# Normalising on Pool by add and multiply, modulation weights queued behind two token tiles, and a new order

**Chip, cores, metric.** One core of one Trainium2 chip. The metric is the device time of one execution in microseconds (us). Executions of one kernel scatter by about 1%, so medians are quoted, and kernels are compared by a ratio: the mean time of one kernel's fast runs over that of the other's fast runs of the same rounds, so not quite the ratio of the quoted medians. One experiment round shares one chip; the kernel before was run again in each.

## The reference

A transformer block with adaptive layer norm, sliding-window attention and an MLP over the token axis; S = 2048 tokens, D = 512, 32 heads of 16, window 256, F = 1792, all bf16.

```python
sa, ca, ga, sb, cb, gb = split(silu(c) @ w_mod)          # six vectors of 512
h = layernorm(x) * (1 + ca) + sa                         # norm l1
x = x + ga * (attention(h @ wqkv) @ wo)                  # causal, last 256 keys
h = layernorm(x) * (1 + cb) + sb                         # norm l2
x = x + gb * transpose(gelu(layernorm(h)^T @ w1 + b1) @ w2 + b2)   # norm l3
```

## The kernel before

The engines are called as in the profile: PE is TensorE (matmuls; PEld its weight loads), DVE VectorE, ACT ScalarE, Pool GpSimd, and SP (SyncE) issues most of the transfers (DMA). The kernel records some 1350 small operations and emits them in a fixed order, a list of numbers with the engine as a letter (A, D, P for ACT, DVE, Pool). Every engine then works through its own queue in that order: in the trace of the change the input of PE's transposition of the silu is ready at 5.85 us, and it starts at 7.31, behind the 14 products listed ahead of it. Tokens come in 16 tiles of 128, four tiles to a group G. Scores are exponentiated on ACT in 75 pieces (`et`), attention products go to `pxy`, projections to `pq` (queries, keys) and `pv` (values, copied into the cleared tiles `VT`), the first MLP product to `pu`. Each tile is normalised three times: `xn` before the projections, `n2` (also called xn) before the second modulation, `hb` before the MLP.

```python
    for v in (0, 1):       # modulation weights of the first norm, 512 KB each
        o_wm[v] = load(f"wm{v}", wmod[:, :, v*D:(v+1)*D], wm_v[:, :, v*D:(v+1)*D], 512 * KBT, -29.0 + 0.1 * v, eng="ACT")
    for t in range(2):     # two token tiles, 128 KB each, on SP's queue
        o_x[t] = load(f"x{t}", xres[t][:], x_dram[t*P:(t+1)*P, :], 128 * KBT, -30.0 + 0.01 * t)
    ...
        def e_rs(e, a, b):                   # 1/std on ACT
            mv, rs = box[box_key]
            ac.activation(out=rs[:, a:b], in_=mv[:, a:b, 1], func=ACT.Ln, bias=eps_t[:], scale=1.0)
            ac.activation(out=rs[:, a:b], in_=rs[:, a:b], func=ACT.Exp, scale=-0.5)
    ...
    def normalize(e, dst, src, key, i):      # on DVE or Pool, as the order says
        mv, rs = box[key]
        (ve if e == "DVE" else po).tensor_scalar(
            out=dst, in0=src, scalar1=mv[:, i, 0:1], scalar2=rs[:, i : i + 1],
            op0=ALU.subtract, op1=ALU.mult,
        )
    # VT[r] cleared by DVE or Pool:
    vt_zero = [op("vz", {"DVE": 1.7, "POOL": 4.3}, lambda e, r=r: (ve if e == "DVE" else po).memset(VT[r][:], 0.0), pos=-20.0 + 5 * r) for r in range(3)]
    ...  # keys split by parity, on Pool: multiply and add
    (ve if e == "DVE" else po).tensor_scalar(out=dst, in0=view, scalar1=mask_par[:, par : par + 1], scalar2=0.0, op0=ALU.mult, op1=ALU.add)
```

The softmax here doesn't subtract the row's maximum and nothing guards it: scores larger than these inputs give would overflow.

Of the kernel before, what the change touches and what calls it, by code (L numbers as in the profile page):

```python
# [45 lines left out]
48 3 0 4 45 2 55 78D 7 1 35 8 39 5 47 6 31 9 82 56 41 81 10 37 11 57 32 12 58 43 13 36 14 83 50 15 34 16 59 84 54 17  # L46
60 18 46 61 42 88D 19 63 89D 20 62 21 92 22 64 33 23 95 93D 53 94D 24 97A 40 96D 38 25 104 85 105 26 107 106A 108 27
52 109A 110D 28 111 86 29 112 30 183 113A 114D 119 87 120 122 184 121D 123 49 124D 130 131 310 125 115 126 132A 116
185 90P 187 118D 117A 134 135 136 188 91P 127 137D 128 44 129D 138 133 139 98 140D 189 195 99D 141 101 100D 196 51
142 103D 186 102D 190 311 143 144 191 203 197 145D 161 312 192 162 204 65 163D 193 146 165 66 147 164 211 205 80P  # L50
148D 194 212 149D 198 313 174 177 175 178 199 176D 218 179D 200 154 213 201 155 219 202 157D 150 151 156D 206 180
314 152D 181 158 220 159 153D 222 207 208 160D 169 223 209 170 166 74 167 171D 210 182 214 315D 224 226 316D 168D
215 317P 67 227 79P 318D 323 68 324 216 234 228 217 319 326D 235 320 221 325D 225 322D 229 522 236 238 230 69 321D
239 172 71 173 70 240 245 72 231 339 75 246 340 232 362 342D 363 341A 523 249 247 330 364D 250 331 327 332D 328 524
334 251 253 354 329D 254 355 525 335 233 356D 526 261 255 336 357 262 343 338D 358 344 337D 237 333 241 263 345D 265
242 346D 351 243 754 266 370 371 244 352 372D 376 267 353D 373 248 377 252 366 256 347 365 257 380 378 374 348 381
359 360 258 384 382 259 76 385 260 350D 264 268 349D 269 392 77 386 361D 367 393 368 73 992 272 369D 375 993 273 994
270 527D 396 996 394 271 528P 997 274 397 379 995 383 529P 755 998 387 530D 388 403 398 284 275 404 276 531 277 532
389 407 405 390 535 534D 408 536 391 533D 395 537D 399 285 409 411 400 538D 281 412 282 278 283 279 401 413 419 280
539 420 402 540 286 566 756 423 421 567 424 287 406 541D 410 414 288 757 430 425 289P 542 568D 431 543 563 544D 564  # L60
415 290D 432 434 291P 416 555 435 556 417 565D 418 422 292D 758 558D 438 293P 436 557D 551 439 552 546 426 553D 294P
427 554D 446 440 579 295P 301 447 559 296P 580 428 450 581D 448 560 297D 451 571 429 298D 572 302 457 452 573D 433
458 562D 437 441 299D 561D 442 300P 461 459 303 574 462 569 575 547 443 465 463 444 304 466 445 449 453 576D 548 454
577 467 473 550D 455 545 487 474 488 456 578 549D 460 464 305 468 475 477 308D 306D 469 484 478 489 309P 485 307P
582 486 583 470 570 479 588 587 471 759D 589 472 476 760D 496 480 761P 493 481 584D 590 762P 593 482 490 591 594 483
497 491 492 598 595 494 599 495 498 607 600 592 608 499 767 763 768 601 764 500 612 596 609 613 501D 597 502D 602
770D 503P 765D 603 620 614 769D 504P 621 766D 513 783 586 787 615 604 625 505D 622 784 610 626 788 785D 585 605 786D
630 627 606 506D 631 611 789D 507P 616 790D 617 639 628 632 795 508D 640 774 633 775 796 623 618 509D 644 641 619
510P 797D 645 624 629 514 511P 634 776D 635 652 646 512P 771 515 653 772 777 773D 642 636 657 654 637 779 516 658
638 780 647 1000 782D 517 662 659 643 518D 520D 663 648 521D 1001 519D 781D 649 671 664 1005 672 1002 1003 1006  # L70
1004D 650 676 673 665 1007 677 798 660 1008 799 651 655 684 678 1009D 656 685 661 674 666 679 716 800D 667 689 668
801 1011 686 669 717 690 778 670 718 675 802 680 694 691 1016 695 692 1012 687 1017 681 703 696 1013 704 1014 697
1018 1019 1015D 682 708 705 683 791 1020D 709 792 688 794D 693 706 698 710 820 793D 699 719 821 720 811 721 812 700
825 822 813D 806 826 701 807 711 702 808D 707 823 827 830 728 712 831 814 828 815 803 713 816D 714 839 832 804 818
715 725 840 805D 819 809 726 824 833 844 841 829 727 817 845 834 729 810 722 723 835 1022 724 836 852 846 1023 730
853 1024 1027 731 1025 854 857 847 1028 1026D 858 1029 855 1033 837 1030 842 732 862 1032 859 733D 838 1021 863 843
734D 1010 1031D 848 1034 735D 849 736D 871 864 1038 737D 872 865 1035 1039 1040 738D 850 739D 876 873 860 1036 877
1041 851 740P 1037D 856 861 745 741P 878 866 884 1042D 867 1044 885 746 1045 1049 742D 1050 868 747 886 889 1051 869
890 1046 874 1052 743D 1047 744D 891 879 894 1048D 870 895 875 748 880 1055 1053D 881 903 749 892 1056 882 750D 1060
896 752D 1061 904 751D 1057 883 1058 887 1062 1059D 905 1063 753D 908 1064A 1065 897 1077 1054 909 948 1043 949 999  # L80
1078 950 910 916 1079 888 917 893 960 898 951 906 899 952 918 911 921 961 953 1080 922 968P 1081 1083 1082 969P 1084
900 962 926 923 1086 970P 927 901 1087 1085 902 907 919 963 980 912 935 913 1088 1066 928 1067 936 929 1068 1069
971D 1089 924 914 1090 1070A 915 972P 940 937 1091 920 941 938 925 930 973D 1092 982 931 1095 932 1093 942 933 1096
981 943 934 939 1094 944 988D 1097 1098 945 1119 1122 983 1099 1128 946 1101 1127 989P 1100 1102 947 954 1103 955
1150 956 957 958 964 1071 1072 959 965 1073 966 974P 1074 1104 1076 975D 1105 967 1123 976D 1142 1075A 1120 977D
1134 1126 1106 978P 1138 1121 1107 984 1124 1108 1129 1110 979D 1130 985 1109 1125 1111 990P 1133 1162 986 1131 1113
1132 1114 1112 987 1146 991D 1116 1115 1135 1147 1136 1143 1139 1137 1117 1140 1163 1151 1141 1144 1166 1148 1167
1154 1118 1149 1170 1152 1158 1159 1153 1174 1145 1155 1178 1156 1182 1179 1160 1186 1161 1164 1175 1171 1157 1190
1165 1200 1168 1201 1169 1172 1210 1211 1173 1176 1212 1187 1180 1183 1181 1213 1184 1202 1177 1230 1240 1188 1220
1189 1203 1250 1185 1231 1221 1222 1214 1204 1191 1205 1223 1192 1251 1224 1193 1270 1194 1252 1195 1206 1241 1196  # L90
1242 1197 1215 1232 1198 1253 1207 1260 1254 1208 1271 1233 1209 1261 1199 1234 1280 1272 1273 1225 1216 1274 1217
1226 1281 1227 1262 1235 1218 1282 1219 1290 1236 1300 1237 1275 1276 1243 1283 1244 1245 1263 1264 1265 1284 1285
1301 1246 1291 1247 1255 1310 1238 1320 1248 1239 1302 1256 1228 1249 1303 1257 1229 1266 1304 1267 1321 1330 1277
1292 1311 1268 1305 1278 1286 1293 1258 1322 1312 1287 1259 1331 1279 1294 1269 1295 1313 1332 1296 1306 1297 1314
1333 1307 1315 1298 1323 1316 1288 1299 1324 1334 1317 1289 1340 1308 1325 1326 1309 1335 1327 1341 1336 1318 1342
1337 1343 1319 1344 1328 1345 1338 1346 1347 1339 1329 1348 1349
# [55 lines left out]
def kernel(  # L152
# [173 lines left out]
    for v in (0, 1):  # L326
        o_wm[v] = load(f"wm{v}", wmod[:, :, v * D : (v + 1) * D], wm_v[:, :, v * D : (v + 1) * D], 512 * KBT, -29.0 + 0.1 * v, eng="ACT")
# [134 lines left out]
    def norm_ops(tag, tiles, deps, poss, box_key, parts):  # L462
        st_ops, rs_of = [], {}

        def e_stat(e, i):
            if i == 0:
                box[box_key] = (
                    small.tile([P, 4, nc.vector.BN_AGGR_DIM], F32, name="mv", tag=tag + "mv"),
                    small.tile([P, 4], F32, name="rs", tag=tag + "rs"),
                )  # L470
            st = small.tile([P, nc.vector.BN_STATS_DIM], F32, name="st", tag=tag + "st")
            ve.bn_stats(out=st[:], in_=tiles(i)[:])
            ve.bn_aggr(out=box[box_key][0][:, i, :], in_=st[:])

        def e_rs(e, a, b):
            mv, rs = box[box_key]
            ac.activation(out=rs[:, a:b], in_=mv[:, a:b, 1], func=ACT.Ln, bias=eps_t[:], scale=1.0)
            ac.activation(out=rs[:, a:b], in_=rs[:, a:b], func=ACT.Exp, scale=-0.5)

        for i in range(4):  # L480
            prev = [st_ops[-1]] if st_ops else []
            st_ops.append(op(f"{tag}st", {"DVE": 0.82}, lambda e, i=i: e_stat(e, i), deps=deps[i] + prev, pos=poss[i]))
            for a, b in parts:
                if b == i + 1:
                    o = op(f"{tag}rs", {"ACT": 0.46}, lambda e, a=a, b=b: e_rs(e, a, b), deps=st_ops[:], pos=poss[i])
                    for k in range(a, b):
                        rs_of[k] = o
# [641 lines left out]
```

## Time and profile before

| | before |
|---|---|
| median of its runs | 285.25 us (three runs, 283.94 to 286.07; 284.8 with a fourth) |
| span of the profiled run | 282.6 us |
| PE, DVE, ACT, Pool busy | 88%, 74%, 66%, 34% |
| normalisations on Pool, each | 2090 ns (14), 2147 ns (4) |
| modulation product starts | 9.73 us |

In the profile a row has engine, operation, output and inputs, and how often it occurs (x14). "Idle before" is the engine's wait ahead of these instructions, and the arrow names what ended it. An engine that is 34% busy can still set the time: what counts is who waits for it. Six of Pool's normalisations, 12.4 us, stand in the chain that ended last. The lines themselves are shown in the prediction.

### The profile page before, as it was taken

The numbers are of one execution on the slowest core, as the hardware profiler recorded it, in microseconds if no ns is written. First come the engines' busy times: TensorE is split into PE (matmuls) and PEld (weight loads), VectorE is DVE, ScalarE is ACT, GpSimd is POOL, SyncE is SP. The second block draws the span as 40 slices with busy tenths as digits, with TensorE's granted clock in tenths as the row PEclk, the third lists the DMA queues.
The fourth block names the chain that finished last, engine by engine and source line by source line (L and its number), as shares of the span: only waits on it lengthen the run. The fifth ranks groups of instructions, "written<-read, shape, count | busy, mean of one in ns | idle before, by whom it ended". The sixth has DMA issues, their size and how long they took to land.

```text
span 282.6 us, 10503 instructions
## 1 busy us (share of the span) xinstructions
PE 249.7 (88%) x4693; PEld 140.1 (50%) x4737; DVE 209.7 (74%) x428; ACT 186.5 (66%) x279; POOL 96.1 (34%) x132
## 2 busy tenths in 40 slices
PE   8787969999699998665799999999799999999993
PEld 2464746656557664442455444545444444444441
DVE  7464998858677779999786889988988770332765
ACT  2074988999679999995999999899832661000000
POOL 8745790344007559695020041105226000000000
PEclk9797999999979999999999999999999999999999
DMA  7997000002930000000000006219057960010222
GB/s 197 345 348 155 6 2 3 2 5 68 295 91 5 5 5 3 2 2 2 2 3 2 5 2 177 52 35 266 3 173 280 410 252 2 0 56 0 98 73 74
DMA packets 31445, 24.80 MB, mean 88 GB/s; under 512 B 6056, under 2 KB 29608, under 8 KB 31400
## 3 DMA queue, kind: packets, MB, share of 16 engines
q1 hardware_dynamic: 30336, 23.08, 27.1%
q10 hardware_dynamic: 1064, 1.05, 1.2%
q8 instruction: 37, 0.61, 0.9%
q14 instruction: 8, 0.07, 0.1%
HBM read 22.03 MB, written 2.10 MB: 85 GB/s over the span
## 4 chain that ended last, share of the span: by engine, by line
PE 54%; DVE 18%; ACT 12%; POOL 8%; issue 4%; DMA 3%; POOLq 0%; DVEq 0%
PE pu L192 27%; ACT et L192 9%; PE pxy L192 8%; PE pq L192 6%; PE psa L192 6%; POOL xn L192 4%; DVE VT L192 4%; DVE et L192 3%; PE pa L192 3%; POOL h L192 2%; DMA wmod<-in_w_mod_dram 2%; DVE xn L192 2%; DVE h L192 2%; PE pv L192 2%; ACT lz L192 2%
## 5 line engine op out<-in xcount | busy, mean ns | idle before, releaser
L192 ACT ACTIVATE et<-psa 128x1536 bf16<-128x1536 f32 x75 | 109.0, 1453 | 11.5 <-PE psb L192 6.4
L192 PE MATMUL pu<-hb,w1p 128*128 128x512 bf16 x213 | 52.2, 380 | 2.0 <-DMA w1p<-in_B_w_dram 0.7
L192 PE MATMUL pu<-guT,w 128*128 128x512 bf16 x219 | 48.4, 379 | 0.3
L192 ACT ACTIVATE et<-psb 128x512 bf16<-128x512 f32 x75 | 44.8, 598 | 0.0
L192 PE MATMUL pxy<-et,VT 128*32 128x192 bf16 (+3 forms) x960 | 37.7, 235 | 6.4 <-DVE OT L192 5.5
L192 POOL TENSOR_SCALAR KT<-kb,mask_par 128x512 bf16<-128x512 bf16 (+1 forms) x36 | 23.1, 655 | 56.4 <-DVE kb L192 52.8
L192 POOL TENSOR_SCALAR xn<-x,mv,rs 128x512 bf16<-128x512 bf16 x14 | 29.2, 2090 | 36.4 <-ACT rs L192 34.3
L192 PE MATMUL pxy<-et,ones_bd 128*32 128x192 bf16 (+3 forms) x960 | 37.8, 234 | 0.0
L192 PE MATMUL pq<-h1T,wqkv 128*128 128x512 bf16 (+1 forms) x147 | 33.7, 343 | 2.9 <-DVE VT L192 1.6
L192 PE MATMUL psa<-QT,KT 32*128 32x192 bf16 (+3 forms) x720 | 30.3, 233 | 5.8 <-ACT et L192 4.9
L192 PEld LDWEIGHTS <-w 128*128 128x128 bf16 x224 | 21.9, 98 | 26.4
L192 PEld LDWEIGHTS <-w1p 128*128 128x128 bf16 x224 | 20.1, 98 | 26.3 <-issue 3.0
L192 PEld LDWEIGHTS <-VT 128*32 128x32 bf16 x960 | 24.7, 97 | 13.0 <-issue 11.6
L192 DVE SCALAR_TENSOR_TENSOR o<-pu,b2FM,bc_gb 128x512 f32<-128x512 f32 x16 | 11.8, 749 | 24.3 <-PE pu L192 24.1
L192 PE MATMUL psb<-QT,KT 32*128 32x192 bf16 (+3 forms) x240 | 29.7, 234 | 0.0
L192 DVE TENSOR_TENSOR et<-et,maskt 128x512 bf16<-128x512 bf16 (+2 forms) x56 | 28.0, 532 | 2.2 <-ACT et L192 2.2
L192 PEld LDWEIGHTS <-KT 32*128 32x128 bf16 x960 | 15.4, 93 | 28.0 <-issue 25.6
L192 PEld LDWEIGHTS <-ones_bd 128*32 128x32 bf16 x960 | 23.6, 98 | 0.1
L192 DVE CAST VT<-pv 64x512 bf16<-64x512 f32 x29 | 19.8, 688 | 3.2 <-PE pv L192 2.7
L192 DVE BATCH_NORM_STATS2 st<-x 128x6 f32<-128x512 bf16 x32 | 21.7, 679 | 0.2
L192 PEld LDWEIGHTS <-wqkv 128*128 128x128 bf16 x160 | 14.0, 100 | 15.2 <-issue 5.3
L192 PE MATMUL pv<-wqkv,h1T 128*32 128x256 bf16 x512 | 17.8, 274 | 1.2 <-DVE VT L192 0.6
(90 smaller groups left out, 353.2 us busy)
## 6 DMA issues: line engine op xcount, KB each, us to landing
w1p<-in_B_w_dram SPq DMA_DIRECT2D x14, 512.0 KB, 6.4
w<-in_B_w_dram SPq DMA_DIRECT2D x14, 512.0 KB, 8.8
x<-in_A_x_dram SPq DMA_DIRECT2D x16, 128.0 KB, 6.4
wmod<-in_w_mod_dram SPq DMA_DIRECT2D x4, 512.0 KB, 6.9
out_dram<-otile SPq DMA_DIRECT2D x16, 128.0 KB, 1.7
wmod<-in_w_mod_dram ACTq DMA_DIRECT2D x2, 512.0 KB, 5.7
wqkv<-in_A_wqkv_dram SPq DMA_DIRECT2D x2, 384.0 KB, 6.1
wqkv<-in_A_wqkv_dram SPq DMA_DIRECT2D x1, 512.0 KB, 7.1
```

The source lines that it names most:

```text
L192: ins = call(*args, **kwargs)
```

## The change

Its intent: Pool had been given normalisations in the belief that they cost 0.7 us there. The change gives Pool a form that does cost about that (add the negated mean, multiply by 1/std), computes the negated means `nm`, corrects the costs, derives a new order of all operations from them, and moves the two weight loads to the queue of the token tiles.

```diff
-        o_wm[v] = load(..., 512 * KBT, -29.0 + 0.1 * v, eng="ACT")
+        o_wm[v] = load(..., 512 * KBT, -29.0 + 0.1 * v)
...
+        def e_nm(e, a, b):
+            mv, _, nm = box[box_key]
+            (ve if e == "DVE" else po).tensor_scalar(
+                out=nm[:, a:b], in0=mv[:, a:b, 0], scalar1=-1.0, scalar2=0.0, op0=ALU.mult, op1=ALU.add)
...
     def normalize(e, dst, src, key, i):
+        mv, rs, nm = box[key]
+        if e == "DVE":
+            ve.tensor_scalar(out=dst, in0=src, scalar1=mv[:, i, 0:1], scalar2=rs[:, i : i + 1], op0=ALU.subtract, op1=ALU.mult)
+        else:
+            po.tensor_scalar(out=dst, in0=src, scalar1=nm[:, i : i + 1], scalar2=rs[:, i : i + 1], op0=ALU.add, op1=ALU.mult)
...
-op("xn", {"DVE": 0.325, "POOL": 0.7}, ...)
+op("xn", {"DVE": 0.325, "POOL": 0.77}, ...)
...   # likewise n2, hb; two-input c2, s2: POOL 1.0 -> 1.17; the last group's l2, l3 kept off Pool, but hb allowed there
...   # ORDER: a new list throughout; VT's first clearing 78D -> 78P
```

## The prediction

> **What bounds the kernel now.** I read the busy times first, then the same by stretch, then the costliest forms on Pool, then the chain that ended last, and last the queues around its longest pieces.
>
> ```profile
> PE 249.7 (88%) x4693; PEld 140.1 (50%) x4737; DVE 209.7 (74%) x428; ACT 186.5 (66%) x279; POOL 96.1 (34%) x132
> ```
>
> PE is busy for 249.7 of 282.6 us. No matmul is added or removed, so the time is about PE's work plus PE's idle time, 32.9 us. The stretches show where that lies (columns: stretch and length, PE, PEld, DVE, ACT, POOL busy, granted clock, DMA share, GB/s):
>
> ```profile
> 0.00:9.70 9.70, 6.63 (x17) 2.15 (x17) 6.35 (x16) 2.09 (x4) 8.67 (x49) 1.00 0.84 240
> 14.00:40.00 26.00, 22.74 (x545) 15.88 (x546) 19.11 (x40) 19.86 (x31) 16.81 (x15) 0.93 0.53 141
> 112.00:131.00 19.00, 11.45 (x326) 7.58 (x327) 17.81 (x35) 17.25 (x23) 15.63 (x10) 1.00 0.01 2
> 131.00:165.00 34.00, 31.06 (x765) 17.57 (x771) 27.98 (x61) 31.37 (x44) 5.56 (x8) 1.00 0.01 3
> 205.00:219.30 14.30, 13.73 (x119) 6.27 (x119) 11.91 (x27) 4.35 (x16) 6.98 (x4) 1.00 0.66 231
> 219.30:278.20 58.90, 58.62 (x267) 26.50 (x271) 30.67 (x47) 10.52 (x15) 0.40 (x1) 1.00 0.28 108
> ```
>
> After 205 us PE is full (72.4 of 73.2 us): nothing another engine does there matters. Before 9.7 us PE runs only warm-up products. The loss in between is largest at 112 to 131 us: 7.55 us idle, while DVE, ACT and Pool are nearly full. Elsewhere ACT is the closest rival (31.37 of 34.0 us).
>
> Pool's forms (last columns: busy us, mean ns, idle before):
>
> ```profile
> L192 POOL TENSOR_SCALAR xn<-x,mv,rs 128x512 bf16<-128x512 bf16 x14 | 29.2, 2090 | 36.4 <-ACT rs L192 34.3 <-DVE x L192 2.1
> L192 POOL TENSOR_SCALAR KT<-kb,mask_par 128x512 bf16<-128x512 bf16 x24 | 17.4, 740 | 46.0 <-DVE kb L192 42.4 <-PE psa L192 3.6
> L192 POOL TENSOR_SCALAR hb<-h,mv,rs 128x512 bf16<-128x512 bf16 x4 | 8.6, 2147 | 7.8 <-ACT rs L192 7.8
> L192 POOL TENSOR_SCALAR KT<-kb,mask_par 128x256 bf16<-128x256 bf16 x12 | 5.7, 486 | 10.4 <-DVE kb L192 10.4
> ```
>
> One operation on tiles of one size costs 740 ns as multiply and add (KT) and 2090 or 2147 ns as subtract and multiply. The old order of instructions had been laid out believing 0.7 us for the latter (the diff shows that figure). The chain (start, us, what) has both parts of the change in it:
>
> ```profile
> 2.86 6.82 DMA wmod<-in_w_mod_dram
> ...
> 18.36 0.92 POOL KT L192 x2
> 19.28 2.06 POOL xn L192
> 21.34 0.46 POOL KT L192
> 21.80 2.07 POOL xn L192
> ...
> 38.06 3.47 DVE xn L192 x2
> ...
> 119.27 2.07 POOL xn L192
> ```
>
> The queues explain two long DVE pieces (first Pool, then DVE, twice; then PE):
>
> ```profile
> 37.39 3.51 POOL L192 MEMSET VT<- 128x4096 bf16 x1
> 37.98 3.55 DVE L192 TENSOR_SCALAR xn<-x,mv,rs 128x512 bf16<-128x512 bf16 x2
> 128.82 1.74 POOL L192 TENSOR_TENSOR h<-h,bc_sb 128x512 bf16<-128x512 bf16 x1
> 127.65 3.20 DVE L192 TENSOR_TENSOR et<-et,maskt 128x1536 bf16<-128x1536 bf16 x2
> 131.69 0.29 PE L192 MATMUL pxy<-et,VT 128*32 128x256 bf16 x4 [3.12 <-DVE OT L192]
> ```
>
> A pair of normalisations on DVE that otherwise takes 0.8 us took 3.55 while Pool cleared VT; two mask products, 0.95 us each elsewhere, took 3.20 beside Pool's two-input add, and PE then stood 3.12 us.
>
> [...]for KT: (740 - 486) / 256 = 0.99 ns an element,[...] with 232 ns fixed; the two-input products took 1210 to 1249 ns. [...]the two weight blocks issued from ACT's queue landed at 9.7 us, when 240 GB/s x 9.7 us = 2.3 MB had moved, although they and the two token tiles are 1.3 MB.
>
> **The change part by part.**
> Start: the weights now follow two token tiles on the one queue, so 1.31 MB are ahead of everything else. By the rates of the single microseconds (36, 253, 258, 318, 241, 267 GB/s from 1 to 7 us) 1.37 MB have moved at 7.0 us. The other input, sT, was ready at 7.6 us behind a 1.76 us clearing of VT on DVE, which moves to Pool. So the modulation product starts near 7.0 instead of 9.73: -2.7 us on the chain. DVE's statistics and masks on Pool (edges done at 9.8) are ready for it.
>
> Normalising on Pool: in the changed program's queues 19 (6 xn, 6 of the second norm, 7 hb) instead of 18. Estimate for the new form: KT's 0.74 to 0.77 us, as it too is one input, two operations; that both scalars are now columns is the uncertain point. Pool loses 18 x 2.1 = 37.8 and gains 19 x 0.75 = 14.3 us; two-input products fall from 14 to 7 (-8.6), a third clearing of VT comes (+3.5), and four of the eleven small negations (+0.8): 96.1 becomes about 68 us. But only what is on the chain counts: six pieces of xn there, 12.4 us, at most 6 x 1.33 = 8.0 us. The two at 19 to 24 us gate the second half of the first projection: -2.7, less 0.7 because the clearing of VT now ends near 16.0, a little after the first kb could be there. Those at 92, 119 and 193 us lie where ACT or DVE have their own queues: half, -2.0. The one at 212 is beside a full PE: 0.
>
> Contention: half as many two-input instructions on Pool: -1.0 of the 3.1 us wait at 131 us. The stretched pair at 38 us may recur, as two clearings still lie near the second projection: 0.
>
> DVE: seven more products at 0.45 (+3.15), one normalisation less (-0.4), seven negations at 0.16 (+1.1), two VT and two part copies from ACT at 0.69 (+2.7), two h1T to ACT (-1.1), VT's clearing away (-1.8): +3.7 us, and it was busy 157 of 191 us from 14 to 205: I charge 0.5.
>
> The sum: -2.7 - 2.7 + 0.7 - 2.0 - 1.0 + 0.5 = -7.2 us, so 278.0.
>
> **The rivals.**
> One: ACT takes over. By the same view of stretches it is busy 169 of the 191 us from 14 to 205, and from 88 us on it idles only about 9. For: faster Pool work cannot shorten exponentials. Then only the start and the first 40 us pay: about 280.5.
> Two: DVE becomes the bound, with 3.7 us more in a stretch that is 6 to 10 us shorter. Against: about 161 of 183 us is 88%. For: at 112 to 131 it was at 94% already, and an in-order queue that runs late delays VT and OT. About 281 to 282.
> Three: the new order is simply truer. The old one was laid out believing 18 Pool instructions cost 1.4 us less each; with right costs PE's 7.55 us at 112 to 131 may nearly vanish as well. About 274.
> Four: adding a negated mean costs as much as subtracting. Then only the start pays, and the order is again wrong: 283. Against: KT's multiply and add.
> Work is also moved between stages: after the last attention product 336 matmuls stand instead of 324, 12 x 0.219 = 2.6 us. That is no cost in itself, but attention must end over 2.6 us earlier before anything is gained.
>
> **Range and chances.** The sure part is the start and the first projection, about 4.7 us; the rest depends on how the waits rearrange. So 273.5 to 282.5. Faster by over 2% means under 279.5, which is 1.5 us above my number: 0.68; within 2%: 0.30; slower: 0.02.
>
> **What would show it.** Pool's normalisations near 750 ns, Pool about 68 us; the modulation product at about 7 us and the first projection about 2.7 us earlier; the transposes at 25 us some 5 us earlier; PE's idle at 112 to 131 clearly below 7.5 us; PE full after the last attention product. I am wrong if the new form takes 2 us, if the weights do not land before 9 us, or if ACT shows the same end of its exponentials with more idle time in front.

The sum: -2.7 - 2.7 + 0.7 - 2.0 - 1.0 + 0.5 = -7.2 us, so 278.0.

## The result, and the profile after

| | before | after |
|---|---|---|
| median | 284.8 us (4 runs) | 274.51 us (273.14 to 275.87, 4 runs) |
| ratio of fast runs | | 0.9635 (95%: 0.9563 to 0.9707) |
| span of the profiled run | 282.6 us | 271.3 us |
| Pool busy | 96.1 us | 68.5 us |
| modulation product starts | 9.73 us | 7.73 us |

The time fell inside the stated range, and the gain (10.3 us by the medians) was larger than the 7.2 us forecast. First the busy times:

```profile
PE 251.4 (93%) x4737; PEld 137.8 (51%) x4737; DVE 208.6 (77%) x442; ACT 184.8 (68%) x277; POOL 68.5 (25%) x131
```

PE's work is the same, and its idle time fell from 32.9 to 19.9 us. But the trace of before lacks 44 matmul records, which makes it look idler than it was. new_again, a second trace of the change that lacks 43, has 270.1 - 244.6 = 25.5 us idle, and is the fairer comparison. By stretch (columns as before: length, PE, PEld, DVE, ACT, POOL, clock, DMA, GB/s):

```profile
112.00:131.00 19.00, 15.08 (x467) 9.60 (x466) 18.51 (x46) 18.85 (x28) 7.22 (x9) 1.00 0.01 3
131.00:165.00 34.00, 33.65 (x706) 17.56 (x706) 27.78 (x62) 33.46 (x47) 5.26 (x7) 1.00 0.07 19
```

The stage at a given clock time is no longer the same one, but PE's hole of 7.55 us at 112 to 131 us has become 3.92 us, and from 131 us on ACT is full (33.46 of 34.0 us). Pool's forms:

```profile
L193 POOL TENSOR_SCALAR xn<-x,nm,rs 128x512 bf16<-128x512 bf16 x12 | 9.5, 790 | 17.9 <-ACT lz L193 10.1 <-ACT rs L193 7.8
L193 POOL TENSOR_SCALAR hb<-h,nm,rs 128x512 bf16<-128x512 bf16 x7 | 5.7, 826 | 6.8 <-ACT rs L193 3.9 <-DVE et L193 2.9
```

2.1 us became 0.8. The chain that ended last (start, us, what):

```profile
1.29 6.09 PE pxy L193 x14
7.81 0.87 PE ps_fm L193 x32
...
13.53 2.19 DVE nm L193
...
34.47 3.36 DVE xn L193
...
48.93 2.47 issue
...
198.31 68.65 PE pu L193 x318
```

No Pool normalisation is among its longest pieces any more, nor the weight transfer. What stands there instead: 14 warm-up products ahead of the modulation product, two DVE instructions of 2.19 and 3.36 us that take 0.16 and 0.40 us elsewhere, and 2.47 us in which PE waits for nothing that the profile shows.

Where in the program the time was won is read best from ACT's 75 exponential pieces, which stand in one sequence in every version. The lead over the kernel before (start of the n-th piece there minus start here, us, worked out from ACT's timeline) for this and two experiments told below (old_addmul: the form alone in the old order; chain_six: the form in six of 18 places):

| piece | 0 | 5 | 10 | 15 | 20 | 25 | 40 | 45 | 60 | 74 |
|---|---|---|---|---|---|---|---|---|---|---|
| the change | 2.8 | 5.1 | 5.5 | 2.2 | 2.1 | 5.3 | 5.4 | 9.2 | 9.6 | 11.8 |
| old_addmul | 0.2 | 3.5 | 4.8 | 4.8 | 4.8 | 5.9 | 6.1 | 8.0 | 8.0 | 7.5 |
| chain_six | 0.1 | 3.4 | 1.9 | 1.9 | 1.9 | 1.7 | 2.1 | 2.8 | 2.8 | 2.3 |

Up to piece 0 the start pays, up to piece 10 the first two projections, at 45 a wait near 131 us. The dip at 15 to 20 begins with the 2.47 us wait; the kernel before has a similar one later, at 75 us, so the lead returns.

Not all of these steps are the kernel's work: PE's granted clock differs between the traces. The profiles of before, after, old_addmul and chain_six show it in 40 slices of the span, in tenths of full speed:

```profile
PEclk9797999999979999999999999999999999999999
PEclk9999999899999999999999999999999999999999
PEclk9799999999999999999999999999999999999999
PEclk9899979999979999999999999999999999999999
```

In the clock records of the packed traces each lower digit is a stretch of 3.4 us at half clock: from 10.4, 24.1 and 78.7 us in before, from 51.6 in the change, from 10.2 in old_addmul, from 11.3, 38.6 and 76.2 in chain_six. In the twelve fast traces 14 such stretches (one of them 6.8 us) lie before PE's last product. Each begins within 2 us of the end of a wait of PE of over 1.5 us, but only about half of those 27 waits have one. So a wait may cost more than itself: of the change's dip of 3.3 us from piece 10 to 15, some 1.9 us go with the stretch at 51.6: new_again, with a wait of 2.04 us and no stretch, dips by 1.4.

The times follow the clock too. 39 executions of the kernel before (leaving out one at 324.78 us, clock 0.752) run from 281.23 us at a mean clock of 0.991 to 289.2 us at 0.962; a line through them gives 2.5 us per 0.01. Fast runs of old_addmul have 0.991 where those of before have 0.977, so by this slope (an estimate) 3.5 of its 9.9 us come with the clock. Some of such a difference belongs to the change: the traces of all five kernels that issue the weights from ACT's queue have a stretch that begins at 9.9 to 11.4 us, those of the seven others none before 48 us. How much of the rest does, no run separates.

### The profile page after: what moved, and what is told of

Same layout as the page of the kernel before. It is cut to its first block, busy times and chain, and to the rows that moved or that the text cites. A ratio compares the mean times of both kernels' runs of the same rounds, so it can differ in the third digit from the quotient of the medians.

```text
span 271.3 us, 10569 instructions
## 1 busy us (share of the span) xinstructions
PE 251.4 (93%) x4737; PEld 137.8 (51%) x4737; DVE 208.6 (77%) x442; ACT 184.8 (68%) x277; POOL 68.5 (25%) x131
## 4 chain that ended last, share of the span: by engine, by line
PE 73%; ACT 11%; DVE 11%; issue 4%
PE pu L193 35%; PE pxy L193 12%; ACT et L193 10%; PE pq L193 8%; PE psa L193 8%; PE pa L193 4%; PE pv L193 3%; DVE st L193 2%; DVE xn L193 1%; ACT lz L193 1%; DVE VT L193 1%; PE pt L193 1%; DVE et L193 1%; DVE nm L193 1%; PE ps_b L193 1%
## 5 line engine op out<-in xcount | busy, mean ns | idle before, releaser
L193 PE MATMUL pu<-hb,w1p 128*128 128x512 bf16 x224 | 53.0, 380 | 0.1
L193 PE MATMUL pu<-guT,w 128*128 128x512 bf16 x224 | 49.2, 379 | 0.0
L193 PE MATMUL pq<-h1T,wqkv 128*128 128x512 bf16 (+1 forms) x160 | 35.8, 350 | 2.2 <-DVE kb L193 1.3
L193 PEld LDWEIGHTS <-VT 128*32 128x32 bf16 x960 | 23.5, 97 | 7.8 <-issue 6.2
L193 DVE TENSOR_TENSOR et<-et,maskt 128x512 bf16<-128x512 bf16 (+2 forms) x56 | 23.8, 461 | 1.5 <-ACT et L193 1.4
L193 DVE CAST VT<-pv 64x512 bf16<-64x512 f32 x31 | 21.1, 686 | 2.9 <-PE pv L193 2.6
L193 PEld LDWEIGHTS <-ones_bd 128*32 128x32 bf16 x960 | 23.0, 97 | 0.1
L193 PEld LDWEIGHTS <-wqkv 128*128 128x128 bf16 x160 | 13.4, 99 | 14.7 <-issue 5.3
L193 DVE CAST QT<-pq 128x512 bf16<-128x512 f32 (+1 forms) x19 | 12.7, 670 | 5.8 <-PE pq L193 5.7
```

The costliest lines, as they stand in the source:

```text
L193: ins = call(*args, **kwargs)
```

## The experiments

Three things changed together: the form on Pool, the queue of the weights, and the order (with the engines it chooses). With the kernel before as one corner and the change, run again, as another, six kernels fill the cube of these.

### The form alone, in the old order

```diff
 # before.py, ORDER untouched; normalize on Pool:
+        if a not in done:      # once per group, on Pool just ahead
+            po.tensor_scalar(out=nm[:, a:b], in0=mv[:, a:b, 0], scalar1=-1.0, scalar2=0.0, op0=ALU.mult, op1=ALU.add)
+        po.tensor_scalar(out=dst, in0=src, scalar1=nm[:, i:i+1], scalar2=rs[:, i:i+1], op0=ALU.add, op1=ALU.mult)
```

> The kernel before with its order of instructions untouched; only Pool's 18 normalisations become add and multiply, each group's negated mean being made on Pool just ahead (11 small instructions of about 0.2 us). Theory A (the form pays by itself, in any order): the six normalisations on the chain give back 1.3 us each less about 0.4 us for the negations, so 5 to 8 us off, 277 to 280 us. Theory B (the new order of instructions pays, and the old one cannot use a faster Pool): under 3 us off, 282 us or more. Pool's busy time about 74 us under both.

Measured: 274.9 us against 285.93 us, ratio 0.9661 (0.9585 to 0.9737). The medians are 11.0 us apart, but three of the nine runs of before were slow; the means of the fast runs are 9.9 us apart. Pool was busy 74.0 us. Theory B falls: the old order could use the faster Pool fully, and even more than theory A said. The lead table says where: 3.3 us from piece 0 to 5 (the two normalisations before the second half of the first projection save 2 x 1.31 = 2.6 us, and the half-clock stretch at 24.1 us, which follows a wait of 1.83 us before, is gone with that wait), 1.3 to piece 10, 1.9 at 45, and the rest after the last piece. The 1.1 around 25 are not the form's: before has a half-clock stretch at 78.7 us after its 1.82 us wait, and this execution has none after its 2.05 us wait. The 1.3 us to piece 10 are an interesting case. Here is Pool's queue, then DVE's (start, us):

```profile
31.90 0.76 POOL L192 TENSOR_SCALAR xn<-x,nm,rs 128x512 bf16<-128x512 bf16 x1 [0.26 <-POOL nm L192]
32.60 3.51 POOL L192 MEMSET VT<- 128x4096 bf16 x1
```

```profile
34.45 2.30 DVE L192 TENSOR_SCALAR xn<-x,mv,rs 128x512 bf16<-128x512 bf16 x2
```

The same Pool normalisation took 2.07 us before. It was on no chain, but it stood ahead of the clearing of VT, and the clearing holds off the DVE pair, which takes 0.8 us elsewhere. With the normalisation 1.3 us shorter the clearing ends earlier relative to DVE, and the pair takes 2.30 us instead of 3.55.

### The queue alone, and both, in the old order

```diff
-        ... 512 * KBT, -29.0 + 0.1 * v, eng="ACT")
+        ... 512 * KBT, -29.0 + 0.1 * v)
-48 3 0 4 45 2 55 78D 7 1 35 8 39 ...
+48 3 0 4 1 2 45 55 78D 7 35 8 39 ...
```

> The kernel before with only the two blocks of modulation weights moved to the queue of the token tiles, behind the first two. Theory A: the modulation product starts near 7.7 instead of 9.7 us, as in the changed kernel, and all 2 us arrive at the end: 282.8 us. Rival (the start is caught by the next wait, Pool's masks and its two 2.07 us normalisations, before the second half of the first projection): the product is earlier, but the transposes at 24 to 25 us start where they did and the time stays at 284.5 us.

Measured: 282.65 us, ratio 0.9912 (0.9824 to 0.9999), which points to theory A, but the interval nearly reaches 1. Its profiled execution is unusable: it took 1113.59 us, so its start could not be read. PE's products of 512 columns took 1217 ns (first MLP product) or 1639 ns (projections) instead of 380 and 391, while the granted clock read 1.00 and ACT kept its pace (1450 ns for the larger part of an exponential piece, 1453 in before); the first execution of new_submul, 479.81 us, is of the same kind (668 ns). Why, no run shows; both were left out as slow.

> Both of these in the old order. Theory A: the sum of the two alone, 7 to 10 us off, 275 to 278 us, so that the new order as such gives no more than 3 us. Theory B: at most 4 us off, 281 us or more, and the new order gives the other 6 us. If the two parts help each other (the start gated by Pool's normalisations), more than the sum of the two alone.

Measured: 272.8 us, ratio 0.9563 (0.9484 to 0.9642). So the queue gave 2.1 us on top of the form by the medians (1.0 point of the ratio, 2.8 us by the means of fast runs), and the first exponential started at 13.37 instead of 16.64 us. Theory A holds: form and queue add up. And this kernel, in the old order, is as fast as the change.

### The new order alone

```diff
 # after.py, ORDER untouched
-            po.tensor_scalar(out=dst, in0=src, scalar1=nm[:, i:i+1], scalar2=rs[:, i:i+1], op0=ALU.add, op1=ALU.mult)
+            po.tensor_scalar(out=dst, in0=src, scalar1=mv[:, i, 0:1], scalar2=rs[:, i:i+1], op0=ALU.subtract, op1=ALU.mult)
-        ... -29.0 + 0.1 * v)
+        ... -29.0 + 0.1 * v, eng="ACT")
```

> The changed kernel with both parts undone and its order kept: Pool subtracts and multiplies again (its negated means are still computed, and not read), and the modulation weights are issued from ACT's queue. Only the order, the engines chosen and the clearing of VT on Pool differ from the kernel before. Theory A: no faster than before, 283 to 286 us, since 19 long normalisations now lie where 0.77 us each was planned. Theory B: most of the gain is still there, 277 to 279 us.

Measured: 285.31 us, ratio 1.0017 (0.9952 to 1.0081). The new order by itself gains nothing. The traces show where it goes: with the fast form and the early weights, the last exponential piece starts at 188.4 us in the new order (new_again) and at 192.3 in the old (old_both), but from there to the end the new one takes 81.8 us and the old 78.8. The 12 matmuls moved behind attention take back most of what is won in front of them.

### Undoing one part of the change

new_submul undoes the form alone, new_actq the queue alone (the two halves of the last diff), new_again is the change itself on their chip.

> The changed kernel with one thing undone: Pool's 19 normalisations subtract and multiply again. If the form is worth the same in both orders (11 us in the old one: 274.9 against 285.9), this lands at 283 to 285 us against 274.5 for the changed kernel. If the new order had been the one that needs it less, 278 to 281 us.

> The changed kernel with the other thing undone: the two modulation weight blocks come from ACT's queue again. If the start arrives at the end unchanged: 2 us more, 276.5 us, with the modulation product at 9.7 instead of 7.7 us. If the start is hidden behind Pool's masks and the clearing of VT up to 15.7 us in this order: less than 0.7 us more.

> The changed kernel as it is, on the same chip as its two undone forms, so that the differences are taken on one chip. 273 to 276 us, ratio 0.960 to 0.967.

| | subtract, ACT's queue | subtract, behind the tokens | add, ACT's queue | add, behind the tokens |
|---|---|---|---|---|
| old order | 1 (before) | 0.9912 | 0.9661 | 0.9563 |
| new order | 1.0017 | 0.9938 | 0.9620 | 0.9561 (and 0.9635 in the first comparison) |

Medians of the new row: 285.31, 284.32, 275.42, 273.6 us. Each interval is about 0.006 to 0.009 wide on either side, so single differences under 1% are weak; but every pair says the same. The form is worth 3.4 to 4.0 points (10 to 11 us), the queue 0.6 to 1.0 (2 to 3 us), the order nothing that shows.

### Which forms are fast on Pool

Nine forms on 128x512 bf16 tiles in Pool's idle tail of the changed kernel, four times each, writing over tiles no longer read; one execution, read for the durations alone. The source tells them apart: x is subtract and multiply by two columns, bc_ga add and multiply, bc_cb multiply and add, bc_sb subtract and multiply by constants, bc_gb multiply and subtract, OT add and subtract, hb multiply and maximum.

> The changed kernel with nine forms of one Pool instruction on 128x512 bf16 tiles, four times each, put on Pool's idle tail (they overwrite hb tiles after their last use; the result stays right). If the subtraction is the cost: every form with a subtraction takes about 2.1 us (subtract and multiply by columns, by constants, multiply and subtract, add and subtract), and those with add, multiply or maximum about 0.77. If the pair is[...]: multiply and maximum takes 2 us too. If it is the two columns of scalars together with the mean's stride: the new subtract and multiply by contiguous columns would be at 0.8. A two-input subtraction as the two-input addition, 1.16 us, or near 2 if subtraction is slow everywhere.

```profile
L193 POOL TENSOR_SCALAR hb<-OT,nm,rs 128x512 bf16<-128x512 bf16 x4 | 9.4, 2342 | 0.0
L193 POOL TENSOR_SCALAR hb<-hb,rs,nm 128x512 bf16<-128x512 bf16 x4 | 8.8, 2189 | 0.0
L193 POOL TENSOR_SCALAR hb<-x,nm,rs 128x512 bf16<-128x512 bf16 x4 | 8.6, 2156 | 19.4 <-PE pu L193 19.4
L193 POOL TENSOR_SCALAR hb<-bc_gb,rs,nm 128x512 bf16<-128x512 bf16 x4 | 8.3, 2083 | 0.0
L193 POOL TENSOR_SCALAR hb<-bc_sb 128x512 bf16<-128x512 bf16 x4 | 7.9, 1966 | 0.0
L193 POOL TENSOR_SCALAR hb<-bc_ga,nm,rs 128x512 bf16<-128x512 bf16 x4 | 3.8, 957 | 0.0
L193 POOL TENSOR_SCALAR hb<-bc_cb,rs,nm 128x512 bf16<-128x512 bf16 x4 | 3.7, 920 | 0.0
```

(mean ns is the number before the last bar). Multiply and maximum is as slow as a subtraction, so it is the pair of operations: add/multiply and multiply/add are fast, the other five forms (four pairs) are not. Columns or constants make little difference (2156 and 1966 ns). A two-input subtraction took 1154 ns and a two-input addition 1264, so subtraction as such is not slow on Pool. Why the pairs differ, no run shows.

### Only the six normalisations on the chain

The prediction had counted six pieces on the chain, and the form gave far more than it said. This run asks whether the other twelve count.

```diff
 # old_addmul, plus:
+        if (key, i) not in ((("l1", 0), 2), (("l1", 0), 3), (("l2", 0), 2), (("l2", 1), 1), (("l2", 3), 0), (("l2", 3), 2)):
+            # as before: subtract, multiply
```

> The kernel before, its order untouched, with add and multiply only in the six Pool normalisations that stand on its chain of waits (the two of the first projection, one each of the second norm's first and second group, two of its last); the other twelve subtract as before. All 18 gave 11.0 us (274.9 against 285.9). If only what stands on the chain counts, as the prediction reckoned, the six give nearly all of it: 275 to 277 us. If the others count too, as they stand in front of something in Pool's queue (one sits ahead of the clearing of VT that holds off DVE at 38 us; two normalisations of 2 us each precede the 3.1 us wait at 131 us), the six give about half: 278 to 281 us, and the waits at 38 and 131 us are still there.

Measured: 279.35 us against 284.59, ratio 0.9819 (0.9761 to 0.9877): 5.2 us, about half of what all 18 gave (9.9 us by the means of fast runs; the 11.0 above takes in slow ones). The intervals of the two ratios do not overlap, so the twelve others do carry something. By the slope of the clock (mean 0.982 here, 0.976 in its runs of before) 1.3 of the 5.2 us go with the clock, which leaves an estimated 3.9 of 6.4. Pool's queue, then DVE's:

```profile
34.04 3.51 POOL L192 MEMSET VT<- 128x4096 bf16 x1
...
119.96 4.54 POOL L192 TENSOR_SCALAR xn<-x,mv,rs 128x512 bf16<-128x512 bf16 x2
124.58 1.38 POOL L192 TENSOR_TENSOR h<-xn,bc_cb 128x512 bf16<-128x512 bf16 x1
126.04 1.74 POOL L192 TENSOR_TENSOR h<-h,bc_sb 128x512 bf16<-128x512 bf16 x1
```

```profile
34.64 3.54 DVE L192 TENSOR_SCALAR xn<-x,mv,rs 128x512 bf16<-128x512 bf16 x2
...
124.87 3.20 DVE L192 TENSOR_TENSOR et<-et,maskt 128x1536 bf16<-128x1536 bf16 x2
```

Both collisions of the kernel before are back. The pair at 34.6 us takes 3.54 us, as before, so the lead does not rise to 4.8 us at piece 10 as in old_addmul. That it falls from 3.4 to 1.9 goes with the clock, which stands at half from 38.6 to 42.0 us here and not there in before. And the two slow normalisations at 120 us push Pool's two products onto DVE's mask products at 125 us; PE again waits 3.11 us for what follows them. In old_addmul the second product ended at 120.3 us, before DVE began the masks at 121.6:

```profile
119.08 1.21 POOL L192 TENSOR_TENSOR h<-h,bc_sb 128x512 bf16<-128x512 bf16 x1
121.60 1.29 DVE L192 TENSOR_TENSOR et<-et,maskt 128x1536 bf16<-128x1536 bf16 x2
```

How long the pair of chain_six is held off can be read from these lines: it starts during the clearing, which ends at 34.04 + 3.51 = 37.55 us, and ends at 34.64 + 3.54 = 38.18 us, 0.63 us later, where a pair that nothing holds off takes 0.8.

### What the change left: the clearing of VT, and a wait without a releaser

```diff
 # fix_vt: after.py, ORDER only
-47 3 0 4 34 1 51 ...                 50 78P 41 ...        143 ...          79P 321D ...
+47 3 0 4 78D 34 1 51 ...             50 41 ...            143 79P ...      321D ...
```

> The changed kernel with the clearings of VT moved: the first goes to DVE at the very start, where DVE idles 1.65 us before the first token tile lands, and one of the two left on Pool is taken 14 us earlier, into Pool's idle time at 20 to 24 us. If a clearing on Pool holds off DVE's column operations between SBUF tiles, the 2.19 us negation at 13.5 us and the 3.44 us normalisation at 34.4 us go back to 0.16 and 0.40 us, and 2 to 4 us arrive at the end: 270 to 272 us. If those stretched instructions were only waiting for something else, their durations stay and so does the time (273.6 us).

Measured: 270.98 us, ratio 0.9540 (0.9485 to 0.9596). Both stretched instructions went back (DVE's queue):

```profile
12.51 0.17 DVE L192 TENSOR_SCALAR nm<-mv 128x2 f32<-128x2 f32 x1
...
33.81 0.43 DVE L192 TENSOR_SCALAR xn<-x,mv,rs 128x512 bf16<-128x512 bf16 x1
```

So the collision was the cause, but little arrived. Against new_again piece 10 starts 2.6 us earlier (39.59 against 42.21 us), and piece 15 only 0.5 (55.66 against 56.20): the wait after it was longer (2.73 us against 2.04), and in this execution PE's clock stood at half from 49.0 to 52.4 us, which it did not in new_again. How much of the clearing's gain arrives is therefore not shown; the ratios, 0.9540 and 0.9561, do not differ clearly.

```diff
 # fix_w1: after.py; the tokens of six w1 loads go behind Pool operations at 65 to 100 us, and
+        if half == 0:
+            po.memset(t[:, 0, 0:1], 0.0)      # the load has to wait for this
         sp.dma_start(out=t[:], in_=w1_v[...])
```

> The changed kernel with six of the seven first w1 loads, which are issued together at 43 to 54 us and needed from about 124 us, held back one by one: Pool writes one column of each tile first, at places between 65 and 100 us, so that each load waits for that. Theory: PE's wait of 2.0 to 2.5 us at 48.9 to 51.4 us, to which the profile gives no releaser, is PE's own instructions coming late behind these loads, since the kernel before shows the like (1.8 us at 75.4) while its w1 loads run; it then vanishes, and about 2 us arrive at the end: 271.5 us. Rival: it is a wait at that place of the program whatever the loads do; then it stays at 49 to 51 us, and the time too.

Measured: 270.23 us, ratio 0.9524 (0.9473 to 0.9574), about 3 us less than the change by the medians, although the run of that was on another chip and the intervals of the ratios overlap (0.9504 to 0.9619 for the change). The stretch from 48 to 52 us, first of the change (new_again), then here:

```profile
48.00:52.00 4.00, 1.81 (x40) 0.86 (x34) 1.95 (x4) 1.85 (x4) 0.80 (x1) 1.00 1.21 291
```

```profile
48.00:52.00 4.00, 4.00 (x71) 1.63 (x72) 3.94 (x9) 3.46 (x6) 0.64 (x1) 1.00 0.02 4
```

With the loads out of the way PE no longer waits there, while the DVE collisions are still in place (2.18 and 3.44 us). That the loads cause the wait is shown. That it is PE's own instructions coming late rests on the traces: the profile lists a DMA queue for instructions (37 packets, 0.61 MB). In all ten traces with this wait (1.82 us in before, 2.73 in fix_vt) PE resumes 1.3 to 1.6 us after one packet of that queue has landed, always the 7th in the new order and the 12th in the old. In new_again the 7th starts at 48.32 us, here at 46.24, although the 6th started at 42.84 and 42.75. No run changed that queue alone, so it stays likely.

> Both of these and a third: three of the 14 warm-up products in front of the transposition of the silu go behind it, as PE's in-order queue holds it to 7.3 us while its input is ready at 5.9. The sum would be 2 to 4, 2, and up to 0.7 us: 267 to 270 us. If the gains only move the wait to ACT, which is busy 95% from 88 us on, 270 to 271 us.

The third part moves tokens 59, 60 and 61 ahead of three warm-up products and puts two of those behind the transposes. Measured: 268.66 us, ratio 0.9475 (0.9405 to 0.9546), the fastest of all and in the expected range. Piece 10 starts at 39.53 and piece 15 at 51.30 us: here there is neither the wait at 49 us nor a half-clock stretch, and the lead of piece 10 gets through. What the third part gave is not shown: the modulation product started at 6.80 us here but at 6.68 in fix_vt without it, where the warm-up products ran faster (14 in 4.80 us, here 11 in 4.19).

## Why the prediction was right, step by step

**The sum.** Forecast 278.0 (273.5 to 282.5), measured 274.51. The direction and the mechanism of the two main parts were right; the gain was undersized by 3 us. Two things were not in the sum: the normalisations off the chain, and the granted clock, which the prediction showed at 0.93 for 14 to 40 us and gave no term. By the estimate above the clock alone is of the size of the miss, so the two are not told apart in full.

**Start, -2.7: 2 to 3 us, right in size, wrong in one reason.** The prediction said that sT was late because of DVE's clearing of VT, and that the product would start at 7.0 us. The clearing left DVE, and sT was still ready only at 7.68 us: its transposition stands in PE's queue behind 14 warm-up products, which end at 7.38. The weights were no longer what was waited for, as foreseen. But in new_again the same 14 products end at 6.41, the product starts at 6.77, and its second half waits for the second weight block until 8.07: the two limits lie close together.

**The form at 0.75 us: 790 and 826 ns.** The point called uncertain, two columns of scalars, turned out harmless. Rival four fell with it: Pool's busy time came to 68.5 us, as computed.

**"But only what is on the chain counts", -2.7 - 2.0: this step failed.** For the six pieces on the chain the sum was right (4.7 forecast, 5.2 measured in chain_six). But all 18 gave 9.9 us by the fast runs, because the other twelve were not free: an instruction that nobody waits for still delays the next one in its engine's queue (in chain_six the clearing of VT starts at 34.04 us behind a normalisation of 2.07 us, in old_addmul at 32.60 behind one of 0.76). The prediction showed both collisions, at 38 and 131 us, and did not look at what stood in front of them in Pool's queue.

**Contention, -1.0: undersized, and for a wrong reason.** It was to come from fewer two-input products. In old_addmul all 14 remained, and DVE's masks still went from 3.20 to 1.29 us, because the products no longer met them. (The prediction took 0.95 us each as their normal time; the pair takes 1.29.) What counts is when, not how many. The lead there grew by 1.9 us at piece 45.

**VT's clearings, +0.7 and 0.** They did collide again, as said, in one place more than said: the negation at 13.5 us, 2.19 us long, is a new wait of the change's own making.

**DVE, +0.5.** Forecast busy 209.7 + 3.7 = 213.4 us, measured 208.6: the instructions added were there, but the mask products took 4.0 us less in sum (25.8 instead of 29.8), as they no longer met Pool's.

**The rivals.** ACT (one) did fill up from 131 us on (33.46 of 34.0 us), but only after the gain was in. DVE (two) was fuller than before at 112 to 131 us (18.51 of 19.0 us), and yet the time fell. The truer order (three) forecast 274 us, nearly the measured number, and its cause is refuted: in the old order the two parts reach 272.8 us. **The 12 matmuls moved behind attention** cost what the prediction said (2.6 us, to be won back in front). From the last exponential piece to the end the change takes 81.3 us, the old order with the fast form 78.8; before, with 80.8, hid the difference behind waits of its own.

## What to carry to other kernels

Measure the form of an instruction, not its kind: on Pool the same one-input instruction took 0.8 or 2.1 us depending on its pair of operations, and rewriting (x - m) * r as (x + (-m)) * r was worth more than a new order of 1350 operations. When an instruction becomes shorter, follow its whole queue: those behind it start earlier too, and here that decided which of Pool's and DVE's instructions collided (DVE's mask pair took 3.20 us beside Pool's products, 1.29 when it did not meet them). Before reading one trace against another, look at the granted clock of both: here a stretch at half clock in the kernel before looked like a gain (the 1.1 us of old_addmul around piece 25). And when a gain is seen in the middle of the trace but not at the end, compare a milestone that both versions have, piece by piece; the step in the lead names the wait that took it.
